# Second-MLP weights converted during the first MLP and kept in DRAM, and products chained in one PSUM bank

## The chip, the cores and the metric

The kernel runs on one core of a Trainium2 chip. TensorE (PE) multiplies into PSUM; ScalarE (ACT), VectorE (DVE) and GpSimd (POOL) work on tiles in SBUF, the first two also on PSUM; SyncE (SP) issues nearly all DMAs. The engines run side by side, each through its own instructions in a fixed order, and wait for one another by semaphores. The metric is the time of one execution in microseconds on the device; the median of several runs is compared.

## What is computed

Sliding-window attention (4 x 8 heads, 576 positions, window 128) gives 2304 tokens of 512 features. They pass two MLPs of 512 to 2048 to 512, one with an ELU and one with a leaky ReLU between its products:

```python
def _moe_ref(x, w_in, w_out):
    h = x @ w_in
    g = np.where(h > 0.0, h, 1.0 * (np.exp(np.minimum(h, 0.0)) - 1.0))
    return (g @ w_out).astype(np.float32)

def _moe2_ref(x, w_in, w_out):
    h = x @ w_in
    g = np.maximum(0.01 * h, h)
    return (g @ w_out).astype(np.float32)
```

The weights arrive as 64-bit words of two 32-bit halves, and the kernel turns them into fp32.

## The kernel before

**Number format.** Each fp32 operand is split into a high part, which PE's fp32r format holds, and a low rest: ACT copies (the high part), DVE subtracts (the rest). A product is three matmuls, high x high, high x low, low x high (`split_mm`, L256).

**Order.** Work is written down in program order and a scheduler at build time lays out every engine's queue: an instruction may move ahead of earlier ones if its operands and a free buffer allow. Instructions in `keep_in_program_order` stay behind all that was written before them on their engine. All matmuls are pinned so, and on ACT the copies of the transposed scores (`copies`, L438) and the two passes `w_a1` and `w_a2` (together `w_first`, L210) that begin the conversion of a weight tile. The queues of SP, DVE and POOL are in order too once they are laid out.

**MLP1.** It runs over five token blocks J of 512, 256, 512, 512 and 512 tokens. A block has 16 steps c, one for each 128 hidden features: `mlp1_h` (12 matmuls, then exp on ACT, two operations on DVE, a cast to the high part `gh` on ACT, the rest `gl` on DVE), and `mlp1_y` of two steps earlier (12 matmuls). In blocks 0 to 3 the attention of later tokens goes in between, in rounds: blocks 1 to 3 have 8 rounds each, at the start of the even steps. A round (L648 and below) is, on PE, `transposes` of two sets of scores (into the PSUM banks of the tags s1 and h, copied out by ACT), `values` of the round before, and `score_mm` of the next round (into s0 and s1). Blocks 0 to 2 end at about 152, 223 and 335 us, block 3 at 445, block 4 at 526. The weights of MLP1 are converted in block 0 (`w_tick`), which calls for no conversion in the step right ahead of a round.

**MLP2.** Both of its products are done by a scheme of seven products of half-size blocks instead of eight (after Strassen), over three groups of 768 tokens. First come 24 units u, 8 for each group (`unit_a`, `unit_b`, `unit_c`): 7 products of 6 matmuls with 384 columns each, accumulated in three banks, x (products 1, 2), y (6, 7, 4) and z (5, 3), with sums s1, a, b taken out by ACT and DVE; the results go through the leaky ReLU to DRAM (`g2T`). Then `second(n)` runs over 28 steps of 12 matmuls for each group (`SEQ`), its operands prepared four steps ahead by `prepare` (splits on ACT and DVE, differences of activations).

**Weights of MLP2 in the kernel before.** A pair of tiles (`pair_load`, 1 MB) is loaded, converted (`w_first`, a shift and an addition on DVE) and combined. The eight input pairs are converted in block 4 of MLP1, with four sums each on POOL; they stay in SBUF and are split as the units need them (`split_w`). The eight output pairs are converted during the last nine units, their sums are made on POOL (`sums`), and `prepare` splits them in the first group of `second`; one sum goes through DRAM (`s4T`) for want of room.

Of the kernel before, what the change touches and what calls it, by code (L numbers as in the profile page):

```python
# [98 lines left out]
def attention_elu_leaky_kernel(  # L99
# [150 lines left out]
    def weights(layer, c, io):  # L250
        while (layer, c) not in W:
            w_tick(NC * layer)
        w = W[layer, c]
        return w[:, io, 0], w[:, io, 1]

# [391 lines left out]

    for J in range(len(BLK1) - 1):  # L648
# [3 lines left out]
        for c in range(NC):  # L652
# [19 lines left out]
            pend.append((J, [c], g))  # L672
    values_to(NS - 1)
# [5 lines left out]
    S, H1, H2, OP, Xr, F, SUM = {}, {}, {}, {}, {}, {}, {}  # L679
    F_ORDER = [(j, 2 * h + q) for h in range(2) for j in range(2) for q in range(2)]  # L680
    s4T = dram.tile([P, NP2, 2 * P], F32, name="s4T")

    def pair_load(kind, i, home, tag):

        raw = home.tile([P, 2, DM, 2], I32, tag=tag, name="wraw")
        if kind == "in":
            src = w_in2[2 * i:2 * i + 2]
        else:
            j, q = F_ORDER[i]
            src = w_out2[j, 2 * q:2 * q + 2]  # L690
        src = src.bitcast(I32).rearrange("c p (n w) -> p c n w", w=2)
        for c in range(2):
            nc.sync.dma_start(out=raw[:, c], in_=src[:, c])
        raws[kind, i] = raw

    def pair_convert(kind, i):

        k = kind, i
        w_ts(k)
        raw, f = raws.pop(k), mids.pop(k)  # L700
        if kind == "in":
            s = wp.tile([P, 8, 2 * P], F32, tag=f"w{i}", name="s")
            to = s[:, 3:7].rearrange("p i n -> p (i n)").rearrange("p (c n) -> p c n", c=2)
        else:
            j, q = F_ORDER[i]
            h = q // 2
            if q % 2 == 0:
                F[j, h] = wp.tile([P, 4, DM], F32, tag=f"w{2 * h + j}", name="f")
            to = F[j, h][:, q % 2 * 2:q % 2 * 2 + 2]
        dve.tensor_tensor(to.bitcast(I32), f, raw[:, :, :, 0], op=ALU.add)  # L710
        if kind == "in":
            for o, x, y, op in ((0, 5, 6, ALU.add), (1, 0, 3, ALU.subtract), (2, 3, 5, ALU.subtract), (7, 4, 1, ALU.subtract)):
                pool.tensor_tensor(s[:, o], s[:, x], s[:, y], op=op)
            S[k] = s

    def block(i, j, q):

        return F[j, q // 2][:, q % 2 * 2:q % 2 * 2 + 2, i * 2 * P:(i + 1) * 2 * P]

    def sums(n, h):  # L720

        if n not in SUM:
            SUM[n] = wp.tile([P, NP2, 2 * P], F32, tag=f"w{3 + n}", name=f"s{n}")
        for q in (2 * h, 2 * h + 1):
            o = {m: x[:, 2 * q:2 * q + 2] for m, x in SUM.items()}
            x, y, op = {1: lambda: (block(1, 0, q), block(1, 1, q), ALU.add), 2: lambda: (o[1], block(0, 0, q), ALU.subtract),
                        3: lambda: (block(0, 0, q), block(1, 0, q), ALU.subtract),
                        4: lambda: (block(0, 1, q), o[2], ALU.subtract)}[n]()
            pool.tensor_tensor(o[n], x, y, op=op)

    def in_load(p):
        pair_load("in", p, *((wrawp, "wraw") if p % 2 else (l2, "xr")))

    def out_load(k):
        if k < NP2:
            pair_load("out", k, *((wp, "w15") if k % 2 else (wrawp, "wraw")))
# [87 lines left out]
    def unit_a(u):  # L824
        x, y, z = (psp.tile([P, HALF], F32, tag=tg[u % 2], name=nm)
                   for tg, nm in ((("s0", "s1"), "px"), (("h", "c"), "py"), (("y0", "y1"), "pz")))
        product(1, u, x, True)
        s1 = small(glp, "gh", "s1")
        nc.scalar.copy(s1, x)
        product(6, u, y, True)  # L830
        a = small(glp, "gl", "a")
        nc.vector.tensor_tensor(a, y, s1, op=ALU.add)
        product(5, u, z, True)
        ps2[u] = x, y, z, s1, a

    def unit_b(u):
        x, y, z, s1, a = ps2[u]
        product(2, u, x, False)
        c11 = small(glp, "gh", "c11")
        g2_out(u, 0, 0, c11, x)  # L840
        product(7, u, y, False)
        b = small(glp, "gl", "b")
        nc.vector.tensor_tensor(b, y, s1, op=ALU.add)  # L843
        c22 = small(egp, "eg", "c22")
        nc.vector.tensor_tensor(c22, z, b, op=ALU.add)  # L845
        g2_out(u, 1, 1, c22, c22)

    def unit_c(u):
        x, y, z, s1, a = ps2.pop(u)
        product(4, u, y, False)  # L850
        c21 = small(egp, "eg", "c21")
        nc.vector.tensor_tensor(c21, y, s1, op=ALU.add)  # L852
        g2_out(u, 1, 0, c21, c21)
        product(3, u, z, False)
        c12 = small(egp, "eg", "c12")
        nc.vector.tensor_tensor(c12, z, a, op=ALU.add)
        g2_out(u, 0, 1, c12, c12)
# [10 lines left out]
    def raw_load(g, role, q, cell):  # L868
# [5 lines left out]
    W_HOME = {1: ("w8", "w9"), 5: ("w12", "w13"), 6: ("w10", "w11"), 2: ("w0", "w2"), 7: ("w4", "w5"), 4: ("w7", "w6"),  # L874
              3: ("w1", "w3")}
    S4 = {}

    def weight(m, q):
        if m in (1, 2, 4):
            return block(int(m == 4), int(m > 1), q)  # L880
        if m == 3:
            return S4.pop(q)
        return SUM[{5: 1, 6: 2, 7: 3}[m]][:, 2 * q:2 * q + 2]

    def prepare(n):
# [5 lines left out]
        if g == 0:  # L891
            i = {(4, 2): 0, (4, 3): 1, (3, 0): 2, (3, 1): 3}.get((m, q))
            if i is not None:
                S4[i] = egp.tile([P, 2, 2 * P], F32, tag="eg", name="s4")
                nc.sync.dma_start(out=S4[i], in_=s4T[:, 2 * i:2 * i + 2])
            if q == 0:
                A2[m] = [wp.tile([P, NP2, 2 * P], F32R, tag=tg, name="a2") for tg in W_HOME[m]]
            split2(*(x[:, 2 * q:2 * q + 2] for x in A2[m]), weight(m, q))
        cell = {r: RAW4[g, r][q] for r in ("b11", "b12", "b21", "b22") if len(RAW4.get((g, r), ())) > q}
        hi, lo = CELLS[n % len(CELLS)]  # L900
# [18 lines left out]
    def second(n):  # L919
# [4 lines left out]
        chain = {1: "x", 2: "x", 6: "y", 7: "y", 4: "y", 5: "z", 3: "z"}[m]  # L924
        for p in range(2):
            if m in (1, 6, 5) and q == 0:
                tag = {"x": ("y2", "y3"), "y": ("h", "c"), "z": ("s0", "s1")}[chain][p]
                PS2[chain, p] = psp.tile([P, HALF], F32, tag=tag, name="p" + chain)
# [9 lines left out]
    def out_store(g, p, i, k, tile_):  # L938
        r, t0 = (2 * p + i) * P, g * GRP + k * HALF
        nc.sync.dma_start(out=out[r:r + P, t0:t0 + HALF], in_=tile_)  # L940

    def evacuate(g, m, p):
        x, y, z = (PS2.get((c, p)) for c in "xyz")
        if m == 1:
            OUT2["s", p] = small(glp, "gh", "s1")
            nc.scalar.copy(OUT2["s", p], x)
# [27 lines left out]
    for c in range(NC):  # L974
# [11 lines left out]
        if c == 9:  # L986
            x2_load(0)
# [139 lines left out]
```

## Time and profile before

| | us |
|---|---|
| median of 3 runs | 908.93 (907.86 to 910.12) |
| the profiled execution | 912.43 |
| its span in the trace | 910.7 |
| PE busy | 880.4 (97%) |
| DVE, ACT, POOL busy | 638.0, 487.0, 200.3 |

A busy PE is not PE at its peak, since matmuls are pipelined: its pace is read from the time that many matmuls took. What an engine's busy share means is read stage by stage, since the stages have different limits.

### The profile page before, as it was taken

How to read it: one execution, taken by the hardware profiler on the slowest of the kernel's cores; microseconds unless marked ns; L12 is line 12 of the kernel's file. 1: busy time of each engine (PE TensorE's matmuls, PEld its weight loads, DVE VectorE, ACT ScalarE, POOL GpSimd, SP SyncE). 2: the span in 40 equal slices, each digit the busy share in tenths (PEclk: the TensorE clock that was granted, in tenths of full speed). 3: DMA queues.
4: the chain of work that ended last, by engine and by line, in shares of the span. 5: the costliest groups of instructions: out<-in, count | busy, mean ns of one | idle time of the engine just before them, and what ended most of it. 6: DMA issues, size and time to landing. Idle time of an engine off the chain costs nothing. (4 is left out here: it accounts for less than half of the span.)

```text
span 910.7 us, 14397 instructions
## 1 busy us (share of the span) xinstructions
PE 880.4 (97%) x5077; PEld 772.1 (85%) x5077; DVE 638.0 (70%) x1296; ACT 487.0 (53%) x1049; POOL 200.3 (22%) x341
## 2 busy tenths in 40 slices
PE   8999999999999999999999999999988779999998
PEld 5578878998877878788888899999988769899998
DVE  6799865556454454443489667896889999785954
ACT  7888854444343443333366446766788543444442
POOL 5802223322232211221064000000016780000000
PEclk9999999999999999999999999999999899999999
DMA  9941323212110120100355043433688707527101
GB/s 333 340 160 62 116 88 98 65 53 78 40 47 24 44 90 24 47 10 1 102 197 187 1 168 123 164 122 108 222 274 249 237 0 214 179 75 223 50 1 70
DMA packets 65768, 106.72 MB, mean 117 GB/s; under 512 B 5920, under 2 KB 52256, under 8 KB 65568
## 3 DMA queue, kind: packets, MB, share of 16 engines
q1 hardware_dynamic: 65120, 104.75, 34.9%
q10 hardware_dynamic: 576, 1.05, 0.3%
q8 instruction: 40, 0.66, 0.3%
q14 instruction: 32, 0.26, 0.1%
HBM read 76.41 MB, written 29.36 MB: 116 GB/s over the span
## 5 line engine op out<-in xcount | busy, mean ns | idle before, releaser
L136 PE MATMUL h_ps<-x,w 128*128 128x512 f32 (+1 forms) x960 | 214.9, 372 | 0.9 <-ACT x L127 0.5
L136 PEld LDWEIGHTS h_ps<-x,w 128*128 128x128 f32 x960 | 166.0, 188 | 38.8 <-ACT x L127 4.0
L136 PE MATMUL y<-gh,w 128*128 128x512 f32 (+1 forms) x640 | 157.2, 368 | 0.0
L136 PEld LDWEIGHTS y<-gh,w 128*128 128x128 f32 x640 | 113.8, 189 | 20.0
L127 POOL TENSOR_SCALAR_AFFINE_SELECT pt<-pt 128x256 f32<-128x256 f32 (+1 forms) x112 | 45.2, 412 | 213.7 <-ACT pt L441 210.1
L127 POOL TENSOR_SCALAR t<-t,stat 128x128 f32<-128x128 f32 (+3 forms) x160 | 71.7, 461 | 90.5 <-DVE stat L127 86.3
L538 ACT ACTIVATE eg<-h_ps 128x512 f32<-128x512 f32 (+1 forms) x80 | 44.0, 550 | 82.5 <-PE h_ps L136 80.2
L860 ACT CAST cells<-raw 128x768 fp32r<-128x768 f32 x60 | 50.1, 837 | 66.9 <-PE py L136 28.9
L541 ACT CAST gh<-eg 128x512 fp32r<-128x512 f32 (+1 forms) x80 | 46.2, 578 | 73.7 <-DVE eg L540 73.2
L127 ACT ACTIVATE t<-t,stat 128x128 f32<-128x128 f32 (+2 forms) x160 | 62.6, 394 | 42.1 <-DVE t L127 29.6
L136 PE MATMUL py<-x,h 128*128 128x384 f32 x336 | 78.7, 338 | 5.1 <-DVE b L843 5.0
L136 PE MATMUL py<-cells,a 128*128 128x384 f32 x432 | 78.0, 336 | 3.3 <-DVE cells L861 3.2
L542 DVE TENSOR_TENSOR gl<-eg,gh 128x512 fp32r<-128x512 f32 (+1 forms) x80 | 54.3, 679 | 36.6 <-ACT gh L541 36.6
L136 PEld LDWEIGHTS py<-cells,a 128*128 128x128 f32 x432 | 74.9, 188 | 5.2 <-DVE cells L861 5.1
L136 PE MATMUL y<-gl,w 128*128 128x512 f32 (+1 forms) x320 | 78.7, 368 | 0.0
L539 DVE TENSOR_SCALAR eg<-eg 128x512 f32<-128x512 f32 (+1 forms) x80 | 32.9, 412 | 64.1 <-ACT eg L538 62.0
L861 DVE TENSOR_TENSOR cells<-raw,cells 128x768 fp32r<-128x768 f32 x60 | 56.6, 956 | 22.9 <-ACT cells L860 22.4
L136 PEld LDWEIGHTS py<-x,h 128*128 128x128 f32 x336 | 60.6, 190 | 5.8 <-DVE b L843 5.4
L136 PEld LDWEIGHTS y<-gl,w 128*128 128x128 f32 x320 | 56.9, 189 | 10.0
L136 PE MATMUL pz<-cells,a 128*128 128x384 f32 x288 | 55.5, 349 | 7.4 <-DVE cells L861 5.2
L136 PEld LDWEIGHTS pz<-cells,a 128*128 128x128 f32 x288 | 52.4, 197 | 9.4 <-DVE cells L861 6.5
L136 PE MATMUL pz<-x,h 128*128 128x384 f32 x240 | 54.6, 341 | 2.7 <-DVE c L845 1.8
(91 smaller groups left out, 1540.4 us busy)
## 6 DMA issues: line engine op xcount, KB each, us to landing
g2T<-c SPq DMA_DIRECT2D x96, 192.0 KB, 2.0
wraw<-in_w_in SPq DMA_DIRECT2D x32, 512.0 KB, 4.7
wraw<-in_w_out SPq DMA_DIRECT2D x32, 512.0 KB, 6.1
raw<-g2T SPq DMA_DIRECT2D x36, 384.0 KB, 3.9
qkr<-in_kT SPq DMA_DIRECT2D x28, 192.0 KB, 2.7
xr<-x2T SPq DMA_DIRECT2D x3, 1536.0 KB, 7.3
b<-g2T SPq DMA_DIRECT2D x12, 384.0 KB, 5.8
out<-c SPq DMA_DIRECT2D x24, 192.0 KB, 2.3
```

The costliest lines, as they stand in the source:

```text
L127: ins = f(*args, **kw)
L136: tc.keep_in_program_order(nc.tensor.matmul(*args, **kw))
L538: nc.scalar.activation(g[:, :m], ps, AF.Exp)
L539: nc.vector.tensor_scalar(g[:, :m], g[:, :m], 1.0, -1.0, op0=ALU.min, op1=ALU.add)
L541: nc.scalar.copy(hi[:, :m], g[:, :m])
L542: nc.vector.tensor_tensor(lo[:, :m], g[:, :m], hi[:, :m].bitcast(F32), op=ALU.subtract)
L860: nc.scalar.copy(hi, src)
L861: nc.vector.tensor_tensor(lo, src, hi.bitcast(F32), op=ALU.subtract)
```

## The change

- A generator `pair_jobs` converts the eight input and then the eight output pairs during blocks 1 to 3 of MLP1, one piece at the end of each step (`next(jobs)`). It makes the four sums on DVE. An input pair takes two pieces: its sums and its words go to DRAM as fp32 (`sT`). An output pair takes four: its eight blocks are also split there, four at a time, and go to DRAM as high and low parts (`hlT`, in runs of 256 values). The raw words of a pair and the two split tiles share the tag `wraw`, of which there is one buffer.
- Block 4 only loads the finished input weights (`s_load`), and the operands of the first units are made a little earlier.
- The units and `second` accumulate in other banks: x takes products 1, 6, 7 and 4, each time after the running sum was copied out; z takes 5 and 3, and w takes 2 alone. s1, b and c21 are plain copies on ACT, a is a plain copy on DVE.
- `second` loads its weights ready split (`hl_load`, 2 MB for each of seven products); `prepare` no longer splits weights, and the differences of the first group move from POOL to DVE. The loads are spread over the last units.

```diff
+    def pair_jobs():
+        pair_load(PAIRS[0])
+        for n, k in enumerate(PAIRS):
+            kind, i = k
+            following = PAIRS[n + 1] if n + 1 < len(PAIRS) else None
+            yield
+            w_first(k)
+            yield
+            w_ts(k)
+            raw, mid = raws.pop(k), mids.pop(k)
+            dve.tensor_tensor(mid, mid, raw[:, :, :, 0], op=ALU.add)
+            a = mid.bitcast(F32).rearrange("p c (i n) -> p (c i) n", i=2)
+            x12, x21 = (1, 2) if kind == "in" else (2, 1)
+            s = wfp.tile([P, 4, 2 * P], F32, tag="wf", name="sums")
+            dve.tensor_tensor(s[:, 0], a[:, x21], a[:, 3], op=ALU.add)
+            dve.tensor_tensor(s[:, 1], s[:, 0], a[:, 0], op=ALU.subtract)
+            dve.tensor_tensor(s[:, 2], a[:, 0], a[:, x21], op=ALU.subtract)
+            dve.tensor_tensor(s[:, 3], a[:, x12], s[:, 1], op=ALU.subtract)
+            if kind == "in":
+                nc.sync.dma_start(out=sT[:, i, 4:], in_=s)
+                nc.sync.dma_start(out=sT[:, i, :4], in_=a)
+                pair_load(following)
+                continue
+            for o, four in ((0, s), (4, a)):
+                yield
+                t = wrawp.tile([P, 2, 4, 2 * P], F32R, tag="wraw", name="hl")
+                nc.scalar.copy(t[:, 0], four)
+                nc.vector.tensor_tensor(t[:, 1], four, t[:, 0].bitcast(F32), op=ALU.subtract)
+                nc.sync.dma_start(out=hlT[:, :, o:o + 4, i], in_=t.bitcast(F32))
+            pair_load(following)
...
+    jobs = pair_jobs()
     for J in range(len(BLK1) - 1):
...
             pend.append((J, [c], g))
+            if J:
+                next(jobs, None)
...
+    def s_load(p):
+        t = wp.tile([P, 8, 2 * P], F32, tag=f"w{p}", name="s")
+        for o, i, n in ((0, 4, 3), (3, 0, 4), (7, 7, 1)):
+            nc.sync.dma_start(out=t[:, o:o + n], in_=sT[:, p, i:i + n])
+        S["in", p] = t
...
+    def unit(u):
+        if u < NU:
...
+            product(1, u, x, True)
+            s1 = small(glp, "gh", "s1")
+            nc.scalar.copy(s1, x)
+            product(5, u, z, True)
+        if u:
+            x_, z_, a_ = ps2.pop(u - 1)
+            product(4, u - 1, x_, False)
+            c21 = small(glp, "gl", "c21")
+            g2_out(u - 1, 1, 0, c21, x_)
+        if u < NU:
+            product(6, u, x, False)
+            a = small(glp, "gl", "a")
+            nc.vector.tensor_copy(a, x)
+        if u:
+            product(3, u - 1, z_, False)
+            c12 = small(egp, "eg", "c12")
+            nc.vector.tensor_tensor(c12, z_, a_, op=ALU.add)
+            g2_out(u - 1, 0, 1, c12, c12)
+        if u < NU:
+            product(2, u, w, True)
+            c11 = small(egp, "eg", "c11")
+            nc.vector.tensor_tensor(c11, w, s1, op=ALU.add)
+            g2_out(u, 0, 0, c11, c11)
+            product(7, u, x, False)
+            b = small(glp, "gh", "b")
+            nc.scalar.copy(b, x)
+            c22 = small(egp, "eg", "c22")
+            nc.vector.tensor_tensor(c22, z, b, op=ALU.add)
+            g2_out(u, 1, 1, c22, c22)
+            ps2[u] = x, z, a
...
+    def hl_load(m):
+        A2[m] = [wp.tile([P, NP2, 2 * P], F32R, tag=tg, name="a2") for tg in W_HOME[m]]
+        for i in (0, 1):
+            nc.sync.dma_start(out=A2[m][i].bitcast(F32), in_=hlT[:, i, IN_HL[m]])
...
-            split2(*(x[:, 2 * q:2 * q + 2] for x in A2[m]), weight(m, q))
...
-            eng = pool if g == 0 and m != 1 else dve
-            eng.tensor_tensor(cell[o], cell[x], cell[y], op=ALU.subtract)
+            dve.tensor_tensor(cell[o], cell[x], cell[y], op=ALU.subtract)
...
-        chain = {1: "x", 2: "x", 6: "y", 7: "y", 4: "y", 5: "z", 3: "z"}[m]
+        chain = {1: "x", 6: "x", 7: "x", 4: "x", 5: "z", 3: "z", 2: "w"}[m]
```

## Rows read from the trace of the kernel before

**Rows 1.** Stretches by stage: us, busy us (instructions) per engine, clock, DMA.

```profile
151.70:223.30 71.60, 71.60 (x596) 65.10 (x594) 42.44 (x166) 33.51 (x121) 21.24 (x56) 1.00 0.25 75
223.30:335.40 112.10, 112.04 (x651) 89.82 (x651) 55.39 (x186) 45.01 (x144) 26.65 (x70) 1.00 0.15 42
335.40:444.70 109.30, 109.30 (x594) 87.80 (x593) 49.47 (x141) 38.52 (x108) 19.03 (x46) 1.00 0.13 41
...
525.90:667.00 141.10, 140.44 (x810) 140.12 (x809) 111.19 (x176) 93.47 (x170) 0.00 (x0) 1.00 0.47 163
667.00:703.60 36.60, 33.78 (x189) 32.10 (x187) 34.86 (x48) 29.66 (x49) 16.62 (x10) 1.00 0.77 248
703.60:790.75 87.15, 70.13 (x349) 65.43 (x350) 80.17 (x78) 41.61 (x64) 38.48 (x19) 0.92 0.53 166
790.75:907.27 116.52, 116.49 (x673) 116.16 (x671) 84.35 (x103) 46.79 (x60) 0.00 (x0) 1.00 0.27 82
```

**Rows 2.** Timeline (start, duration, engine, line): PE's first product of MLP2.

```profile
525.87 0.51 PE L136 MATMUL px<-x,h 128*128 128x384 f32 x2
```

**Rows 3.** Timeline of PE: the longest wait, in brackets with its releaser.

```profile
708.59 2.29 PE L136 MATMUL py<-x,h 128*128 128x384 f32 x6 [5.04 <-DVE b L843]
```

**Rows 4.** Timeline of ACT, then PE, at a round in block 1.

```profile
177.49 0.41 ACT L541 CAST gh<-eg 128x256 fp32r<-128x256 f32 x1 [0.82 <-DVE eg L540]
178.78 0.81 ACT L441 COPY pt<-pt_ps 128x256 f32<-128x256 f32 x2 [0.88 <-PE av_ps L136]
...
179.02 1.10 PE L136 MATMUL s_ps<-qkr 64*128 64x256 f32 x8
```

**Rows 5.** Timeline of ACT, then PE, at a round in block 2.

```profile
249.84 0.62 ACT L541 CAST gh<-eg 128x512 fp32r<-128x512 f32 x1 [1.22 <-DVE eg L540]
251.79 0.81 ACT L441 COPY pt<-pt_ps 128x256 f32<-128x256 f32 x2 [1.34 <-PE av_ps L136]
...
252.04 1.46 PE L136 MATMUL s_ps<-qkr 64*128 64x256 f32 x12
```

**Rows 6.** Timeline: the second input pair, its load (SP) and conversion in block 4.

```profile
126.86 0.80 SPq L693 DMA_DIRECT2D wraw<-in_w_in  x2
...
454.53 0.63 ACT L541 CAST gh<-eg 128x512 fp32r<-128x512 f32 x1 [1.30 <-DVE eg L540]
455.06 1.14 ACT L182 ACTIVATE wf<-wraw 128x1024 f32<-128x1024 f32 x1
456.10 1.14 ACT L187 ACTIVATE wraw<-wraw 128x1024 int32<-128x1024 uint32 x1
457.64 1.23 DVE L127 CUSTOM_DVE_ANT_0 s<-wraw,wf 128x2048 uint16<-128x2048 uint16 x1 [0.17 <-DVE wf L127]
```

**Rows 7.** Timeline of ACT at a round in block 0.

```profile
92.77 1.10 ACT L441 COPY pt<-pt_ps 128x256 f32<-128x256 f32 x4 [1.75 <-PE av_ps L136]
94.03 1.14 ACT L182 ACTIVATE wf<-wraw 128x1024 f32<-128x1024 f32 x1
```

**Rows 8.** Groups by line: count | busy us, mean ns of one | idle before.

```profile
L861 DVE TENSOR_TENSOR cells<-raw,cells 128x768 fp32r<-128x768 f32 x60 | 56.6, 956 | 22.9 <-ACT cells L860 22.4
L127 DVE TENSOR_SCALAR wf<-wf 128x1024 int32<-128x1024 int32 x32 | 29.1, 910 | 1.1 <-ACT wf L182 1.1
L127 DVE TENSOR_TENSOR t<-t 128x256 f32<-128x256 f32 x48 | 19.4, 425 | 0.6
L829 ACT COPY s<-px 128x384 f32<-128x384 f32 x24 | 11.4, 474 | 4.8 <-DMA g2T<-c 2.4 <-DMA x2T<-ys 1.7 <-PE px L136 0.6
```

**Rows 9.** Landing of a pair's loads; ys, 1 KB runs; `s4T` store; a wait at 657-672.

```profile
DMA to landing us min/median/max: 3.7/4.1/4.6
...
DMA to landing us min/median/max: 4.0/4.1/4.1
...
s4T<-s SPq DMA_DIRECT2D x1, 1024.0 KB, 3.9
...
DVE c L845 <- DMA g2T<-c: 2.8, 1, 2.8
```

More of the change, by code (lines that the diff above doesn't have):

```diff
@@ L254, in weights, with pair_load @@
         return w[:, io, 0], w[:, io, 1]
+    sT = dram.tile([P, NP2, 8, 2 * P], F32, name="sT")
+    hlT = dram.tile([P, 2, 8, NP2, 2 * P], F32, name="hlT")
+    def pair_load(k):
+        if k not in PAIRS:
+            return
+        kind, i = k
+        raw = wrawp.tile([P, 2, DM, 2], I32, tag="wraw", name="wraw")
+        src = w_in2[2 * i:2 * i + 2] if kind == "in" else w_out2[:, i]
+        src = src.bitcast(I32).rearrange("c p (n w) -> p c n w", w=2)
+        for c in range(2):
+            nc.sync.dma_start(out=raw[:, c], in_=src[:, c])
+        raws[k] = raw
+    PAIRS = [(kind, i) for kind in ("in", "out") for i in range(NP2)]
+    def pair_jobs():
+        pair_load(PAIRS[0])
+        for n, k in enumerate(PAIRS):
+            kind, i = k
+            following = PAIRS[n + 1] if n + 1 < len(PAIRS) else None
[24 more added lines that the diff above has]
+            pair_load(following)
     def split_mm(ps, whi, wlo, xhi, xlo, first, last, **kw):
@@ L678, in attention_elu_leaky_kernel @@
     g2T = dram.tile([P, NC, NT], F32, name="g2T")
[L679 to L736, printed above, removed]
+    S, H1, H2, OP, Xr = {}, {}, {}, {}, {}
+    def s_load(p):
[3 more added lines that the diff above has]
+        S["in", p] = t
@@ L1050, in attention_elu_leaky_kernel @@
-    prepare(0)
-    prepare(1)
-    sums(2, 1)
-    sums(3, 1)
-    for h in range(2):
-        sums(4, h)
-    nc.sync.dma_start(out=s4T, in_=SUM[4])
-    unit_c(NU - 1)
-    for q, cell in enumerate(raw_cells(wrawp, "wraw", 2) + raw_cells(l2, "at0", 2)):
-        raw_load(0, "b22", q, cell)
-    for q, cell in enumerate(raw_cells(l2, "at1", 2) + raw_cells(wfp, "wf", 1) + raw_cells(wfp, "wf", 1)):
-        raw_load(0, "b21", q, cell)
-    for n in range(2, AHEAD):
-        prepare(n)
+            continue
@@ new lines, in attention_elu_leaky_kernel @@
+        if p == 1:
+            raw_cells("b11", l2, "xr", 4)
+            xa = quarters(x1p.tile([P, 10, HALF], F32R, tag="x1", name="cells"), 5)
+            CELLS += [(xa[0], xa[1]), (xa[2], xa[3])]
+        elif p == 2:
+            hl_load(1)
+        elif p == 3:
+            raw_cells("b12", wp, "w15", 2)
+            raw_cells("b12", wrawp, "wraw", 2)
+        elif p == 4:
+            hl_load(5)
+        elif p == 5:
+            prepare(0)
+            hl_load(6)
+        elif p == 6:
+            prepare(1)
@@ L1064, in attention_elu_leaky_kernel @@
+    hl_load(2)
+    raw_cells("b22", wp, "w14", 2)
+    hl_load(7)
+    xb = quarters(x1p.tile([P, 10, HALF], F32R, tag="x1", name="cells"), 5)
+    CELLS += [(xb[0], xb[1]), (xb[2], xb[3]), (xa[4], xb[4])]
+    prepare(2)
+    unit(NU)
+    raw_cells("b22", l2, "at0", 2)
+    raw_cells("b21", l2, "at1", 2)
+    for _ in range(2):
+        raw_cells("b21", wfp, "wf", 1)
+    prepare(3)
+    hl_load(4)
+    hl_load(3)
     FROM = {"b11": ("b21", (13, 14, 15, 20)), "b12": ("b12", (16, 17, 18, 19)), "b22": ("b11", (21, 22, 23, 24)),
```

129 lines of the change are left out of this document (28 added, 101 removed).

## The prediction

> **What bounds the kernel now.** I read the time by stages first: TensorE (PE) is busy all of each MLP1 stretch from 151.7 to 444.7 us and all of the second and third token groups of the second MLP's last products (116.49 of 116.52 us), at full granted clock; the one stretch with real gaps is 703.6 to 790.75 us, where PE is busy 70.13 of 87.15 us at a granted clock of 0.92, and VectorE (DVE) 80.17 us [rows 1]. So the kernel is a PE stream with one hole. The size of the hole follows from the pace: the last two groups are 672 products of 384 columns in 116.5 us, 0.1734 each [rows 1]; the second MLP has 24 units of 42 such products and 3 groups of 336, 2016 in all, so 349.5 us. They start at 525.87 [rows 2] and would end at 875.4; they end at 907.27 [rows 1]. **Some 32 us** are lost, which is all that the second MLP can give back. About 3 us of it lie at 667 to 703.6 (PE busy 33.78 of 36.6) [rows 1]; the rest begins with PE waiting 5.04 us for DVE [rows 3] and goes on while ACT, DVE and GpSimd prepare the weights and operands of the first group at the same time.
>
> **The change part by part.**
>
> *The hole.* In the stretch 703.6 to 790.75 the 28 weight splits, the sums on GpSimd, and the last conversions go; 12 subtractions come back to DVE at 0.96 us each, less than the splits took. What is left per group is what the second and third groups do already, and those run without a gap [rows 1]. So the hole closes, except for what is late next: transfers. Seven pairs of prepared weights are 14.7 MB, against 8.4 MB of raw weights and 2 MB of sums before, beside the same 6.3 MB of activations. Before, the DMA engines were 0.77 busy at 667 to 703.6, and one activation store that was late held DVE up for 2.8 us [rows 1, 9]. I leave 8 us of the 32 (bounds 3, today's small stalls alone, and 16, half the hole): **24 us gained**.
>
> *The chain in one bank.* x takes products 1, 6, 7 and 4; between two of them lie two others, 12 x 0.1734 = 2.08 us, in which the copy (0.47 us on ACT, [rows 8]) has to be read out; before there were three or four. In 525.9 to 667 DVE is busy 111 and ACT 93 of 141 us and PE has no gap [rows 1]; the change shifts 0.5 us per unit from DVE to ACT. Cost: none if the reader is at most 1.4 us behind; 0 to 12 us otherwise (half a microsecond per unit). I count 2 of the 8 us above. A page speaks against this edit: the Trainium skill, "Perfetto Trace Analysis", Optimizing Tensor Performance, wants independent matmul groups to rotate through different PSUM banks so that evacuation overlaps the next group. Here two other banks stand between each reuse, so the rows give no cost; by the rule the reuse would be exposed, which is the last rival below.
>
> *The conversion moved into MLP1: where the forecast is decided.* From 444.7 to 525.9 it hid under PE; nothing is gained by taking it out there (PE has no gap to lose in that stretch). It goes to 48 steps from 151.7 to 444.7, where every second step, the even ones, opens with a round of attention. The generator gives an input pair two steps and an output pair four, and with the first load on step 0 the two ACT passes of w_first (pinned in program order) fall on odd steps always: right behind the step's cast of g and right ahead of the next round's copies of the transposed scores, which are pinned behind them. Today these copies come straight after the cast, and PE starts the next scores into the same bank at once: cast 177.49, copies 178.78, scores 179.02 in block 1 [rows 4]; 249.84, 251.79 and 252.04 in block 2 [rows 5]. In block 0, where weights are prepared between rounds, the passes come after the copies (copies 92.77, pass 94.03) [rows 7]. How pinned and unpinned work differ is seen in block 4: the second input pair is loaded at 126.86, some 300 us before block 4, as soon as its buffer is free, but its passes wait for their place, right behind a step's cast: cast 454.53, passes 455.06 and 456.10 (to 457.24) [rows 6].
>
>  So from the start of the cast to the end of the second pass are 2.7 us with 512 columns and, by the shorter cast (0.41 for 0.63), 2.5 with 256; the next may start 0.1 before that end, as the second pass does before the first's. Copies that began 1.29 us after the cast's start (178.78 - 177.49) can now begin at 2.4, those at 1.95 (251.79 - 249.84) at 2.6: PE waits **1.1 us per pair in block 1, 0.65 in blocks 2 and 3**, even when everything has arrived: 8 x 1.1 + 8 x 0.65 = 14 us. Nothing behind it hides this, since PE has no other gap.
>
>  Then the one buffer: raw words of a pair, and the two halves of the split output weights, share the single slot of the pool wraw. An input pair closes a loop: passes 2.2, addition 1.3 with its start [rows 6], SyncE's issues with a 0.5 MB store and the attention loads ahead 1.5, two loads of 0.5 MB that land 4.6 us after the second issue 5.0 [rows 9], 1.0 of queueing in the DMA rings: 11.0 us (bounds 8.7 without any wait, 13 with DVE busy). DVE has 42.4 of 71.6 us in block 1, and seven pairs of 0.91 + 1.23 + 4 x 0.43 [rows 6, 8] bring it to 69, so some waits there are likely. PE's time for the same two steps is 71.6 / 8 = 8.95. The longer of the two sets the pace: 7 x (11.0 - 8.95) + 1.1 = **15.5 us** (9 to 29).
>
>  An output pair: passes 2.2, addition 1.3, four sums 1.7 [rows 6, 8], then twice copy 1.14 (the 1024 columns of a pass, [rows 6]), subtraction 1.3 (0.96 x 1024/768, [rows 8]) and a store of 1 MB, then the load 5.1. The trace has no such store: a 1 MB one with long runs landed in 3.9 us, and two of 256 KB with 1 KB runs, the run length here, in 4.0 to 4.1 [rows 9]. Between 3.9 and twice 4.1 I take 6.0, nearer to the short runs. Sum 27.2, and 3 for six hand-overs between queues that hold attention work (0 to 6): 30.2 us, bounds 23 and 35. PE's four steps are (112.1 + 109.3) / 8 = 27.7 us. 7 x (30.2 - 27.7) + 0.65 = **18 us** (5 to 52).
>
>  Nothing else there costs: POOL loses its sums, stores and loads add some 42 MB over 293 us to 40 to 75 GB/s [rows 1], DVE stays under its limit in blocks 2 and 3 (55 + 4 pairs of 6.4 of 112 us).
>
>  Sum: +15.5 + 18 - 24 = +9.5 us, 922 against the profiled execution's 912.43 (span 910.7 and 1.7 around it). The three runs have their median 3.5 us lower, at 908.93; I carry the difference over: **918 us**.
>
> **Rivals.** *Faster:* the loops through the one buffer close within PE's steps (the transfers land as in the emptier stretches), so only the 14 us of queue order and 2 of small waits are paid, and 28 us are gained: 897. For it: unpinned work floats far ahead in before [rows 6]; against it: the sum of an output pair's own durations is 27 of 27.7 us. It decides at a store of about 5.5 us with 1 us of waits. *Slow buffer:* the output loop takes 35 us, because ACT and DVE stand in order behind a copy that waits for its store: 7 x 7.3 + 15.5 - 24 = +43, 952. It is the slower side of the same mechanism, decided by how stores of 1 KB runs land. *The hole stays:* the prepared weights or activations arrive late at the switch, 20 us stay lost: +21.5, 930. For it the 0.77 of the DMA engines; against it that unpinned loads float. *The bank:* each of the three reuses of x per unit costs 0.3 us, 24 x 3 x 0.3 = 21.6 more, 940; the copies' 0.47 us against 2.08 speaks against it. [...]
>
> **How the numbers follow.** Forecast as above 0.42 (own range 903 to 930), faster 0.28, slow buffer 0.17, hole stays 0.09, bank 0.04. About 0.3%, 2.7 us, is what can be told from no change. Under 906.2: 0.25 of the faster case and 0.04 of the forecast, 0.29; within: 0.03 and 0.09, 0.12; over: the rest, 0.59. The range leaves out a tenth on either side: 896 to 946.
>
> **What would show it.** Right: in the new trace each odd step from 151.7 on has the two passes ahead of the copies, PE's longest waits in that stretch are scores <- ACT copies, some 1 to 3 us, 16 times, the three blocks take some 30 us longer than 293, and from the start of the second MLP to the end it is about 357 us. Queue order alone is right if the waits are 1.1 and 0.65; the buffer if ACT's passes wait for the load of wraw. Wrong: the three blocks take 293 us or little more (the passes would then have to stand elsewhere in ACT's queue), or PE still waits for DVE at the switch.

## The result and the profile after

The changed kernel takes a median of **915.62 us** against 909.85 for the kernel before on the same chips: ratio **1.006, 95% interval 1.0041 to 1.0079**, 5.8 us longer. The forecast was 918 with a range of 896 to 946. One of its 16 executions took 4432 us, at a mean granted clock of 0.18; the ratio leaves it out, and without it the median is 915.09. The profiled execution took 917.84 us, with a span of 916.2.

By stages the profile after reads as follows (us of the stretch, then busy us and instructions of PE, PEld, DVE, ACT and POOL, the granted clock of PE, the DMA engines' share and GB/s). The stretches are blocks 1, 2, 3 and 4 of MLP1, the units (two lines), and the three groups of `second` (two lines):

```profile
151.70:240.00 88.30, 77.44 (x595) 67.45 (x594) 64.92 (x213) 49.77 (x137) 30.17 (x56) 0.96 0.74 251
240.00:356.30 116.30, 114.90 (x651) 90.73 (x650) 76.40 (x217) 60.01 (x160) 35.72 (x70) 1.00 0.47 149
356.30:473.40 117.10, 114.94 (x603) 91.33 (x602) 73.77 (x176) 56.41 (x127) 23.37 (x46) 0.97 0.43 141
473.40:554.30 80.90, 80.36 (x355) 66.20 (x354) 38.50 (x60) 25.94 (x42) 0.00 (x0) 1.00 0.36 117
554.30:700.00 145.70, 142.83 (x807) 142.16 (x806) 103.54 (x159) 98.22 (x189) 0.00 (x0) 0.98 0.51 172
700.00:737.85 37.85, 36.19 (x205) 35.23 (x204) 21.18 (x34) 21.16 (x42) 0.00 (x0) 1.00 0.82 264
737.85:796.09 58.24, 58.24 (x337) 58.24 (x337) 44.12 (x54) 25.71 (x34) 0.00 (x0) 1.00 0.85 288
796.09:912.60 116.51, 116.48 (x672) 116.16 (x671) 80.74 (x97) 48.91 (x64) 0.00 (x0) 1.00 0.27 82
```

Read against [rows 1]: the hole at the switch to `second` is gone (58.24 of 58.24 us busy in its first group), and the 5.04 us wait of [rows 3] with it. MLP2 now lasts 912.6 - 554.3 = 358.3 us where it lasted 381.4: 23.1 us gained. Blocks 1, 2 and 3 last 321.7 us where they lasted 293.0: 28.7 us lost, 16.7 of them in block 1. Block 4 did not get shorter without its conversions: 80.9 us, where the kernel before has

```profile
444.70:525.90 81.20, 81.20 (x360) 67.22 (x359) 62.81 (x79) 43.92 (x60) 27.06 (x32) 1.00 0.36 123
```

The waits that PE's rows show, and what ended them (us in total, times, longest; first over blocks 1 to 4, then over MLP2):

```profile
PE s_ps L136 <- ACT pt L489: 14.3, 13, 2.3
...
PE px L136 <- ACT b L854: 3.3, 3, 1.7
PE px L136 <- ACT s L831: 1.2, 1, 1.2
```

A round of block 1 shows the mechanism, on ACT and then PE (start, duration, engine, line; in brackets the idle time ahead and its releaser):

```profile
203.20 0.41 ACT L589 CAST gh<-eg 128x256 fp32r<-128x256 f32 x1 [0.86 <-DVE eg L588]
204.96 1.12 ACT L182 ACTIVATE wf<-wraw 128x1024 f32<-128x1024 f32 x1 [1.36 <-DMA wraw<-in_w_in]
205.97 1.13 ACT L187 ACTIVATE wraw<-wraw 128x1024 int32<-128x1024 uint32 x1
207.00 0.63 ACT L489 COPY pt<-pt_ps 128x256 f32<-128x256 f32 x2
...
207.41 0.92 PE L136 MATMUL s_ps<-qkr 64*128 64x256 f32 x6 [2.25 <-ACT pt L489]
```

Where [rows 4] have the cast and then the copies, the two passes now stand in between, and they have waited 1.36 us for their words before they began. The copies come 3.8 us after the cast's start, not 1.29, and PE loses 2.25 us. In block 2 (the rows that answer [rows 5]) it is the fp32r copy of the split that stands there in the steps without passes:

```profile
254.61 0.62 ACT L589 CAST gh<-eg 128x512 fp32r<-128x512 f32 x1 [1.22 <-DVE eg L588]
255.61 1.05 ACT L299 CAST hl<-wf 128x1024 fp32r<-128x1024 f32 x1 [0.38 <-DMA hlT<-hl]
256.61 0.81 ACT L489 COPY pt<-pt_ps 128x256 f32<-128x256 f32 x2
```

### The profile page after: what moved, and what is told of

Same layout as the page of the kernel before. It is cut to its first block, busy times and chain, and to the rows that moved or that the text cites. A ratio compares the mean times of both kernels' runs of the same rounds, so it can differ in the third digit from the quotient of the medians.

```text
span 916.2 us, 14526 instructions
## 1 busy us (share of the span) xinstructions
PE 887.4 (97%) x5077; PEld 776.3 (85%) x5077; DVE 620.4 (68%) x1330; ACT 500.5 (55%) x1067; POOL 140.5 (15%) x281
## 4 chain that ended last, share of the span: by engine, by line
PE 82%; DMA 4%; ACT 3%; DVE 2%; issue 2%; SPq 0%; ACTq 0%; DVEq 0%
PE px L136 21%; PE h_ps L136 19%; PE y L136 19%; PE pz L136 10%; PE pw L136 5%; PE s_ps L136 4%; PE av_ps L136 3%; DMA wraw<-in_w_in 1%; PE pt_ps L477 1%; DMA x2T<-ys 1%; DMA g2T<-c 1%; ACT wraw L187 1%; DMA xr<-x2T 1%; ACT pt L489 1%; ACT wf L182 0%
## 5 line engine op out<-in xcount | busy, mean ns | idle before, releaser
L136 PEld LDWEIGHTS y<-gh,w 128*128 128x128 f32 x640 | 113.7, 189 | 21.0 <-ACT ys L617 1.0
L861 ACT CAST cells<-raw 128x768 fp32r<-128x768 f32 x84 | 70.4, 840 | 84.5 <-PE px L136 49.9
L862 DVE TENSOR_TENSOR cells<-raw,cells 128x768 fp32r<-128x768 f32 x84 | 79.4, 956 | 38.2 <-ACT cells L861 37.7
L136 PE MATMUL px<-x,h 128*128 128x384 f32 x432 | 99.7, 337 | 4.5 <-ACT b L854 3.3
L136 PE MATMUL px<-cells,a 128*128 128x384 f32 x576 | 101.8, 334 | 0.0
L136 PEld LDWEIGHTS px<-cells,a 128*128 128x128 f32 x576 | 100.0, 188 | 0.0
L586 ACT ACTIVATE eg<-h_ps 128x512 f32<-128x512 f32 (+1 forms) x80 | 44.1, 551 | 101.0 <-PE h_ps L136 95.5
L127 POOL TENSOR_SCALAR_AFFINE_SELECT pt<-pt 128x256 f32<-128x256 f32 (+1 forms) x112 | 60.4, 557 | 226.1 <-ACT pt L489 224.2
L136 PEld LDWEIGHTS px<-x,h 128*128 128x128 f32 x432 | 77.3, 189 | 6.2 <-ACT b L854 4.3
L752 ACT CAST h<-s 128x512 fp32r<-128x512 f32 (+1 forms) x72 | 49.6, 693 | 26.9 <-PE pz L136 24.6
L136 PE MATMUL s_ps<-qkr 64*128 64x256 f32 (+4 forms) x256 | 45.8, 377 | 14.8 <-ACT pt L489 14.8
L127 DVE CUSTOM_DVE_ANT_0 t<-s_ps,bias 128x256 f32<-128x256 f32 (+4 forms) x160 | 52.2, 369 | 4.8 <-PE s_ps L136 4.2
```

The lines of the kernel that those rows point to most:

```text
L127: ins = f(*args, **kw)
L136: tc.keep_in_program_order(nc.tensor.matmul(*args, **kw))
L586: nc.scalar.activation(g[:, :m], ps, AF.Exp)
L752: nc.scalar.copy(hi[:, a:b], s[:, a + o:b + o])
L861: nc.scalar.copy(hi, src)
L862: nc.vector.tensor_tensor(lo, src, hi.bitcast(F32), op=ALU.subtract)
```

## The experiments

Below, a block's length is the time between VectorE's last copies of `ys` of it and of the block before, and "the units" are the time from the first product of MLP2 to the first product of `second`; at 1008 x 0.1734 us the units hold 174.8 us of products. All medians stand beside 909.6 to 910.3 us for the kernel before, run with them. The four columns on the right are from the one profiled execution of each kernel, which can lie some us off its median: most for e11 (4.7 us longer), e4 (4.4 shorter), e10 (3.5 longer) and e7 (3.2 longer).

| kernel | median us | block 1 | block 2 | block 3 | units |
|---|---|---|---|---|---|
| before | 909.85 | 71.4 | 112.7 | 109.3 | 187.0 |
| after | 915.62 | 88.3 | 116.9 | 116.6 | 183.4 |
| e1 passes in the other step | 917.36 | 89.9 | 121.5 | 110.9 | 184.3 |
| e2 no loads | 908.43 | 80.6 | 117.1 | 115.5 | 181.5 |
| e3 both | 909.94 | 91.0 | 115.7 | 111.2 | 182.1 |
| e8 both, no sums | 909.73 | 88.4 | 115.5 | 110.5 | 182.3 |
| e4 banks of before | 908.20 | 84.8 | 117.1 | 113.3 | 177.2 |
| e5 input pairs in block 4 | 897.33 | 71.4 | 117.0 | 114.7 | 181.0 |
| e6 and pieces in the round | 889.14 | 71.5 | 113.9 | 109.2 | 182.8 |
| e7 and banks of before | 886.25 | 71.5 | 113.8 | 109.3 | 181.8 |
| e9 e6, own tile for ys | 884.36 | 71.5 | 113.9 | 109.3 | 177.8 |
| e10 e7, own tile for ys | 885.74 | 71.5 | 113.9 | 109.3 | 181.1 |
| e11 load first | 919.36 | 95.5 | 116.9 | 115.3 | 182.9 |
| e12 e11, no stores | 909.05 | 83.6 | 116.9 | 113.7 | 184.3 |

(e8 is the time of one execution; the units of before contain its wait of [rows 3].) The four causes held against one another are: the place of the passes in ACT's queue, the loop through the landing buffer, DVE's load, and in MLP2 the chain in one bank.

**e2: the loop taken away.** After the first input pair nothing is loaded: the next pairs take the words that lie there.

```diff
         kind, i = k
+        if kind == "in" and i:
+            raws[k] = last["raw"]
+            return
```

> The raw words of the first input pair are kept and converted eight times, the other seven input pairs are not loaded: the input part of the second MLP's weights is wrong, all other work is the same. The passes stay ahead of the copies. If the buffer's loop (load behind addition) is what made block 1 longer, block 1 falls from 88.3 to 72 to 74 us and the time by 14 or more. If the place in the queue alone costs 1.1 us per pair, block 1 is 80 to 82 and the time falls by 6 to 8, to about 908. Blocks 2 and 3 stay at 232 to 235 by both.

Ratio 0.9985 (0.9973 to 0.9997); 7.2 us less than the changed kernel. The block's window, and PE's waits in it:

```profile
151.70:232.30 80.60, 74.36 (x595) 65.19 (x594) 64.73 (x213) 49.16 (x138) 30.06 (x56) 1.00 0.53 183
```

```profile
PE s_ps L136 <- ACT pt L493: 6.2, 8, 0.9
```

With the words always there, the passes alone still cost block 1 9.2 us, about 1.1 for each of 8 pairs, and no single wait is over 0.9 us. The rest of the 16.9, 7.7 us, goes with the loads; up to 3.5 of it is PE's granted clock, which is 1.00 here and 0.96 in block 1 of the changed kernel.

**e1 and e3: the passes one step later.** In block 1 the generator starts one step later, so that the passes fall into the step that has a round in it and not ahead of one; all later pieces move by a step with them. e3 does it without loads too.

```diff
-            if J:
+            if J > 1 or (J and c):
                 next(jobs, None)
```

> The generator starts one step later, so the two ACT passes of a pair fall on even steps: still behind the step's cast, but no longer right ahead of a round's copies. Block 1 of the changed kernel took 88.3 us against 71.6 before, blocks 2 and 3 233.4 against 221.4. If the place in ACT's queue is the cost, block 1 goes to 72 to 75 us, blocks 2 and 3 to 222 to 226, and the time falls by 20 us or more, to about 893. If the one buffer paces block 1 (10.6 us from pair to pair against 8.95 that PE needs), block 1 stays at 84 to 88 and only blocks 2 and 3 gain, about 7: 908. My theory holds both to be there: the buffer lags 1.65 us per pair, 11.5 over seven, of which one step without a round, about 4.5, can be absorbed: block 1 76 to 80, total about 897.

> Both edits at once: the passes on even steps, and the seven input pairs not loaded (that part of the weights is wrong). If these two causes are all that lengthened block 1, it is 72 to 74 us, and PE waits for no copies there. If it stays above 77, a third cause is at work (VectorE, which has some 65 of 72 us to do, or transfers that come late). The time is about 892 to 895 by the first.

Both ratios say no gain over the kernel before: 1.0099 (1.0065 to 1.0133) and 1.0005 (0.9995 to 1.0015). Block 1 did not shrink, in e3 not even without loads. My expectation of e1 was plainly wrong, and that of e3 too. Part of it is the clock: its mean over block 1 is 0.94 in e1 and 0.92 in e3, where e2 has 1.00, so some 5 and 7 us of these two blocks are a slower PE (estimates, as if PE were busy throughout). PE's waits on `s_ps` disappear and come back at another product, in e3 as

```profile
PE av_ps L136 <- DVE eg L592: 13.2, 7, 2.3
```

The timelines of ACT, DVE and PE at one round of e3 show how:

```profile
192.15 1.16 ACT L182 ACTIVATE wf<-wraw 128x1024 f32<-128x1024 f32 x1
193.21 1.15 ACT L187 ACTIVATE wraw<-wraw 128x1024 int32<-128x1024 uint32 x1
194.26 0.36 ACT L590 ACTIVATE eg<-h_ps 128x256 f32<-128x256 f32 x1
...
194.40 1.23 DVE L127 CUSTOM_DVE_ANT_0 wf<-wraw,wf 128x2048 uint16<-128x2048 uint16 x1 [0.36 <-ACT wraw L187]
195.54 0.29 DVE L591 TENSOR_SCALAR eg<-eg 128x256 f32<-128x256 f32 x1
...
196.08 0.42 DVE L592 TENSOR_TENSOR eg<-h_ps,eg 128x256 f32<-128x256 f32 x1
...
196.55 0.88 PE L136 MATMUL av_ps<-pt,vr 128*64 128x128 f32 x12 [1.20 <-DVE eg L592]
```

The next step's exponential stands behind the passes on ACT, the two DVE operations behind it (the second reads the same hidden sums) stand behind the weight addition, and `av_ps` of the round is released by the second. So in block 1 PE pays for the 2.3 us of passes, and the addition of 1.23 behind them, in either step; only which product pays changes. In blocks 2 and 3 the shift helped, 226.9 us in e3 for 232.6 in e2; why is not shown here.

**e8: DVE's sums.** Three of the four sums of each input pair are left out of e3; both its stores take the words instead.

> The run with shifted steps and without the input loads, and three of the four sums of each input pair left out (that part of the weights is wrong; the stores are as many). There block 1 was 91 us, with PE waiting 14.7 us for VectorE to have read the odd step's bank before the next round's values. If VectorE's queue is the cause, 1.3 us less per pair gives 80 to 84 us and waits of 5 to 9; if the two passes on ACT are (exp of the odd step stands behind them), block 1 stays at 88 to 91.

```profile
PE av_ps L136 <- DVE eg L597: 13.4, 7, 2.3
```

Block 1 is 88.4 where it was 91.0, and the waits are as before: DVE's sums are not what PE waits for.

**e5: the input pairs out of blocks 1 to 3.** They are converted in block 4 again, as in the kernel before, but with their sums on DVE; the generator handles only output pairs.

```diff
-    PAIRS = [(kind, i) for kind in ("in", "out") for i in range(NP2)]
+    PAIRS = [(kind, i) for kind in ("out",) for i in range(NP2)]
...
-            if J:
+            if J > 1:
```

> Undoes one part: the input pairs are converted in block 4 as in the kernel before (sums on VectorE, kept in SBUF), and the generator does the output pairs alone, from block 2 on. If it is the input pairs that lengthened block 1 (88.3 us against 71.6), block 1 is 71 to 73, blocks 2 and 3 stay at 230 to 234, block 4 stays at 80 to 82 with VectorE some 70 us busy, and the time falls by about 16, to 899. Against it: if preparation costs PE the same wherever it stands, block 4 grows by what block 1 gives back and the time stays at 912 to 916.

Ratio 0.9868 (0.9848 to 0.9889). Block 1 is back at 71.4 us, and block 4 stays at 81.0 us: the conversion had been free there. 18.3 us of the changed kernel's time is the input pairs' move; 16.9 of it is seen in block 1. e5 also makes the first units' operands as late as the kernel before does, and its units are 2.4 us shorter.

**e6: pieces behind the copies.** This is e5, and for the even steps the generator's piece is called inside the round, after the copies of the transposed scores. (The first load comes at the end of block 1.)

```diff
-            if J > 1:
+            if J > 1 and c % 2 or J == 1 and c == NC - 1:
                 next(jobs, None)
...
                     w_tick(NC)
+                if J > 1:
+                    next(jobs, None)
```

> As the run before, and the pieces of the even steps stand inside the round, behind the copies of the transposed scores, so the two ACT passes of an output pair come where ACT waits for the next scores (2.2 us in the trace of before). If the place of the passes is what lengthened blocks 2 and 3 by 12 us, they go from 233 to 221 to 225 and the time to about 889. If the one buffer's loop is it, they stay at 230 to 234 and the time at 899; if VectorE's added work is it (some 40 us per block), they stay above 228.

Ratio 0.9775 (0.9749 to 0.9801), another 8.2 us. In ACT's timeline the copies follow the cast again as in [rows 5], and the fp32r copy comes after them:

```profile
251.58 0.62 ACT L589 CAST gh<-eg 128x512 fp32r<-128x512 f32 x1 [1.35 <-DVE eg L588]
253.44 0.81 ACT L489 COPY pt<-pt_ps 128x256 f32<-128x256 f32 x2 [1.24 <-PE av_ps L136]
...
255.39 1.05 ACT L299 CAST hl<-wf 128x1024 fp32r<-128x1024 f32 x1 [0.87 <-DMA hlT<-hl]
```

The output pairs' work is the same, with the same loads, stores and single buffer, so neither the loop's length nor DVE's added work lengthened blocks 2 and 3 by itself. What the loop did there was to hold the fp32r copy longer in front of the transposed scores: in blocks 2 and 3 of the changed kernel ACT waits 4.6 us, in 7 such copies, for the store of the one before. e6 has such waits too (0.87 us above), but behind the copies. Where a wait hides in a record, the group's busy time shows it: the group of `s_ps` products in block 2 (count, busy us, mean ns, idle ahead), in the changed kernel and then in e6, is

```profile
L136 PE MATMUL s_ps<-qkr 64*128 64x256 f32 (+3 forms) x80 | 13.2, 357 | 1.3 <-ACT pt L489 1.3
```

```profile
L136 PE MATMUL s_ps<-qkr 64*128 64x256 f32 (+3 forms) x80 | 10.4, 354 | 0.0
```

2.8 us of busy time and 1.3 of idle make 4.1 of the 4.2 us by which block 2 had grown.

**e4, e7, e9, e10: the units.** In e4 the units' sums lie in the banks of the kernel before (its three functions `unit_a`, `unit_b`, `unit_c` instead of `unit`, so that the small tiles `gh`, `gl` and `eg` are dealt out as there too); e7 is e6 with the same. In e9 and e10, which are e6 and e7 otherwise, the last block's four `ys` tiles have a tile of their own:

```diff
+            own = wrawp.tile([P, NK, n], F32, tag="wraw", name="ysl") if J == len(BLK1) - 1 else None
             for i, y in enumerate(Y.pop(J)):
-                if i == 3:
+                if own is not None:
+                    ys = own[:, i:i + 1]
+                elif i == 3:
```

> The 24 units take their sums as in the kernel before (x for products 1 and 2, y for 6, 7 and 4, z for 5 and 3, three or four products between two uses of a bank instead of two); the rest is the changed kernel. The units took 183.6 us against 174.8 without a gap. If the short chain in one bank is what lost the 8.8 us, they take 175 to 177 and the time falls by 6 to 8, to about 908.5. If late transfers alone lost them (a store of the first MLP's result that took 9 us, weight loads beside stores), the units stay at 181 to 184 and the time within 2 us of the changed kernel's.

> As the run before, and the 24 units take their sums in the banks of the kernel before, with three or four products between two uses. With the units alone changed they fell from 183.6 to about 177 us; if that adds up with the rest, the time is about 883, below both kernels. If the units' gaps came from transfers that have moved by now, the time is that of the run before.

> The version with the input pairs in block 4 and the pieces inside the round took 889.1 us, and its units 182.8 us from the first unit to the first product of the cells, of which 174.8 are products. Here the last block's four ys tiles lie in a tile of their own, so that their stores, which land some 7 us behind the large activation load, no longer hold the buffers that the first unit's VectorE writes. If those stores hold up the units: units about 178 us, time about 885 us. If the chain of products in one bank alone makes the 8 us: units unchanged at 182 to 183 us, time 889 us.

> The version with the units' sums in the banks of the kernel before took 886.3 us, its units 181.8 us, and the last block's ys stores held the units' buffers there as well. With a tile of their own for ys: if the stores and the bank are two separate losses, units 176 to 178 us and time 882 to 884 us; if a later wait (the switch's subtraction behind an activation load) takes their place, units above 180 us and time 886 us.

e4: ratio 0.9992 (0.997 to 1.0015), units 6.2 us shorter. That looks like the price of the chain, and I took it for that until e9: with the chain kept and only the `ys` tiles moved, the units fall from 182.8 to 177.8 and the time to 884.36 (0.9709, 0.9694 to 0.9725). What the first unit ran into is in the changed kernel's rows, on DVE and then PE:

```profile
561.93 0.56 DVE L850 TENSOR_TENSOR c<-pw,s 128x384 f32<-128x384 f32 x1 [3.74 <-DMA x2T<-ys]
...
563.46 1.32 PE L136 MATMUL px<-x,h 128*128 128x384 f32 x6 [1.70 <-ACT b L854]
565.94 1.01 PE L136 MATMUL px<-x,h 128*128 128x384 f32 x2 [1.16 <-ACT s L831]
```

and in the landings (KB each, median us) of the last block's stores and of the load issued ahead of them:

```profile
xr<-x2T SPq DMA_DIRECT2D x2, 1536.0 KB, 8.0
x2T<-ys ACTq DMA_DIRECT2D x2, 256.0 KB, 8.3
x2T<-ys SPq DMA_DIRECT2D x2, 256.0 KB, 9.6
```

The stores hold the buffers that the first unit's sums want; DVE stands 3.74 us, ACT's copies come late, and PE, whose products keep their order, comes to the same bank again two products later. With the banks of before the stores landed as late (8.3 and 9.6 us in the kernel before, 8.3 and 9.5 in e4), and PE waited 1.4 us in all the units of e4, where the changed kernel has 4.5. In e9 they land no earlier either (8.5 and 9.9), but hold no buffer that a unit wants, and PE's waits in the units are

```profile
PE px L136 <- ACT b L872: 1.4, 2, 0.8
PE px L136 <- DVE a L859: 0.4, 1, 0.4
```

so the chain as such costs at most the 3.0 us by which 177.8 exceeds 174.8. The clock had a share here as well: its mean over the units is 0.98 in the changed kernel, 0.99 in e6 and 1.00 in e4 and e9, so that of the 5 to 6 us some 3 are waits and most of the rest is a slower PE. Together the two cures do not add up: e7, expected at 883, is not clear of e6, and e10 (0.9723, 0.9695 to 0.9752) is where e7 is (0.9746, 0.9714 to 0.9778). There another wait sets the units, DVE first and then PE:

```profile
703.07 0.96 DVE L127 TENSOR_TENSOR raw<-raw 128x768 f32<-128x768 f32 x1 [4.16 <-DMA raw<-g2T]
703.95 0.55 DVE L861 TENSOR_TENSOR b<-py,s 128x384 f32<-128x384 f32 x1
...
704.55 1.97 PE L136 MATMUL py<-x,h 128*128 128x384 f32 x5 [4.15 <-DVE b L861]
```

A difference for `second`, whose activations land late, stands in DVE's queue ahead of a sum that PE needs. It is the wait of [rows 3] with another cause.

**e11 and e12: what closes the loop in block 1.** In e11 the next input pair's load is issued behind the addition, ahead of the sums and the two stores; e12 also leaves out the stores of seven pairs.

```diff
             a = mid.bitcast(F32).rearrange("p c (i n) -> p (c i) n", i=2)
+            if kind == "in":
+                pair_load(following)
...
                 nc.sync.dma_start(out=sT[:, i, 4:], in_=s)
                 nc.sync.dma_start(out=sT[:, i, :4], in_=a)
-                pair_load(following)
```

> The changed kernel with one edit: the following input pair's load is issued right behind the addition of the two passes, ahead of the three sums and the two stores. Block 1 took 88.3 us there: some 9 us over the kernel before from the place of the passes in ScalarE's queue alone, and some 8 from the loop through the one landing buffer and the lower granted clock. If the loop sets these last microseconds, it gets some 1.5 us shorter for each pair: block 1 at 82 to 85 us, waits for the landed pair gone, time 911 to 913 us. If the loop does not set them, block 1 stays at 87 to 89 us and the time at 915 us.

> The version with the load ahead of the stores, and seven of the eight input pairs are not stored to DRAM (the first MLP2 product then uses the first pair for all, so the output is not the reference's). With the load first, block 1 took 96.1 us instead of 88.3, since ScalarE's pass waited 7.1 us for the store of the buffer wf, which landed in 7.0 us behind the loads instead of 3.3. If the loop of an input pair closes through two buffers, wraw (its load) and wf (its store), neither the order of load and store nor one of them alone can shorten it, and without the stores only the place of the passes is left: block 1 at 80 to 83 us, no wait of a pass for a store or a load, time 908 to 911 us. If the stores do not matter: block 1 at 88 to 96 us, time 915 to 919 us.

e11 did neither of what was expected: 1.009 (1.0053 to 1.0127), block 1 at 95.5 us (the 96.1 that e12's expectation names counts from a copy earlier). By the time alone it is not clear of the changed kernel, whose interval is 1.0041 to 1.0079, and its profiled execution is a long one, at a low clock in block 1:

```profile
152.03:248.10 96.07, 82.46 (x598) 71.94 (x596) 66.03 (x214) 50.57 (x139) 29.98 (x56) 0.91 0.70 230
```

At 0.91 for 0.96 the clock is some 5 of the 7.2 us by which the block grew. What is shown is that the new order brought no gain. A wait of ACT says why:

```profile
ACT wf L182 <- DMA sT<-wf: 7.1, 5, 2.6
```

and the landings (KB each, median us) go with it:

```profile
wraw<-in_w_in SPq DMA_DIRECT2D x14, 512.0 KB, 5.9
...
sT<-wf SPq DMA_DIRECT2D x8, 512.0 KB, 7.0
```

In the changed kernel the same two views have a wait for the load and a faster store:

```profile
ACT wf L182 <- DMA wraw<-in_w_in: 4.1, 5, 1.4
```

```profile
wraw<-in_w_in SPq DMA_DIRECT2D x14, 512.0 KB, 5.4
sT<-wf SPq DMA_DIRECT2D x8, 512.0 KB, 3.3
```

A pass needs two things: its words in `wraw`, and a free buffer of the tag `wf`, which the pair before holds until it is stored. The rows fit a loop that is closed by whichever of load and store is issued second. Without the stores, e12 is back at 909.05 us (0.9988, 0.9969 to 1.0007), 10.3 below e11 and 6.6 below the changed kernel, and PE waits 7.8 us in block 1, 1.6 at the longest. Its block 1, 83.6 us, is 0.6 above what was expected, and the time is as expected; passes still wait 1.4 us for a store or a load (three times). The reading through two buffers holds so far as it goes: taking away the loads (e2) or the stores (e12) shortens block 1, changing their order does not. How much of e12's gain is the buffer and how much the emptier DMA engines (0.54 busy, for 0.70 in e11 and 0.74 in the changed kernel) it does not tell apart.

## Why the prediction was right, and where not

- **The hole.** 24 us of 32 were to come back; 23.1 did. The 8 us that were to stay did (358.3 - 349.5 = 8.8), but not where I put them: the switch has no gap at all, at a DMA share of 0.82 to 0.85, and nearly all of the loss (183.4 - 174.8 = 8.6) lies in the units.
- **The chain in one bank.** 2 us (0 to 12) were counted. e9 bounds the chain itself at 3.0 us, so the term was about right; the other 5 or so come from a step that I did not make: whose buffers the units' sums take over. The late stores were in the kernel before as well, where PE waited 0.7 us in all for the copies of s1; the change exposed them. The rival that had each reuse exposed at 0.3 us (21.6 us) is refuted. The prediction also read too much into a rule: the Trainium skill, "Perfetto Trace Analysis", Optimizing Tensor Performance, asks that independent matmul groups rotate through different PSUM banks so that the readout of one overlaps the next group. That the reuse would be exposed was my own conclusion: two products in other banks stand between each reuse here, so the readout does overlap the next product. What the runs show is that little is lost while the readers are on time (3.0 us at most), and 6.2 us with the late stores (the changed kernel against e4).
- **The passes ahead of the copies.** 1.1 us a pair were counted in block 1, 8.8 in all, and 9.2 were measured (e2). The longest waits (up to 2.3 us), the releaser and the length of the three blocks (28.7 us more, "some 30" told) are as described; the rows show 13 such waits for the 16 told. In blocks 2 and 3 I counted 0.65 for each of 8 pairs, 5 us; e6 gives 8.2 in the time. What failed there is that I placed only the passes: the fp32r copies of the split stand ahead of the copies of other rounds in the same way.
- **The input pairs' loop.** +15.5 us were told for block 1 and 16.9 measured (13.4 in the profiled execution of e4, whose block 1 is the same code); 18.3 in the time (e5). The loop was put at 11.0 us a pair; block 1 took 88.3 / 8 = 11.0. The loads landed in 5.4 us for the 4.6 that the sum took. No row shows its 1.0 of queueing or its 1.5 of issues by themselves, and the clock's share stands in no term, so that the whole agrees to a tenth is in part luck. The buffer that I closed it through is only one of two (e11, e12).
- **The output pairs' loop** is the step that was wrong. I had 30.2 us for it, longer than PE's 27.7, and took +18 from that. e6 runs the same loop in (113.9 + 109.2) / 8 = 27.9 us, which is PE's pace to within 0.2, so it did not set the pace; the store, put at 6.0 us, landed in 5.3 (4.8 in e6). On this step the faster rival had it right. Blocks 2 and 3 became 11.5 us longer all the same, for the two reasons above and below. In the profile the parts are 16.9 + 11.5 - 23.1 = +5.3 us, where the sum had 15.5 + 18 - 24 = +9.5: a largest cost that was not there was in good part made up by what had been left out, and so far the nearness of 918 is luck.
- **Left out: the clock.** In block 3 PE's granted clock fell, to the lower of its two levels (1.2 and 2.4 GHz) for some us, where PE had just waited (stretches of 5 us):

```profile
355.00:360.00 5.00, 3.68 (x30) 2.59 (x28) 3.11 (x6) 3.82 (x6) 0.00 (x0) 1.00 0.66 249
360.00:365.00 5.00, 4.51 (x12) 3.28 (x13) 4.50 (x16) 2.76 (x12) 1.97 (x4) 0.52 0.42 118
365.00:370.00 5.00, 5.00 (x19) 4.05 (x18) 2.58 (x7) 2.33 (x5) 1.35 (x3) 0.80 0.00 0
```

  and PE's timeline there:

```profile
360.49 1.86 PE L136 MATMUL s_ps<-qkr 64*128 64x192 f32 x6 [1.82 <-ACT pt L489]
362.28 5.20 PE L136 MATMUL h_ps<-x,w 128*128 128x512 f32 x12
```

  Twelve products of 512 columns took 5.2 us; at the pace of [rows 1] they are 12 x 0.1734 x 512/384 = 2.8. If PE was busy all the while, the mean of 0.97 over 117.1 us cost block 3 some 3.5 us, 0.96 over 88.3 block 1 as much, and 0.98 over 183.4 the units about as much again (estimates). Not every wait brings it on: of six stretches of 13 to 15 us in block 1, with eight waits, two show 0.89 and four 1.00. It is not the same in every execution either: e4, whose MLP1 is that of the changed kernel, had block 1 at 84.8 us with a clock of 0.98. And it goes with the times: of the changed kernel's executions the two at a mean clock of 0.996 took 910.7 and 910.8 us, the three at 0.985 to 0.987 took 918.4 to 918.9. PE's gaps are therefore not the whole price of a wait.
- **"Nothing else there costs"** was not borne out for the transfers. Traffic in block 1 went from 75 to 251 GB/s, the DMA share from 0.25 to 0.74, and a pair's loads landed in 5.4 us for 4.1 [rows 9]. What that cost by itself no run tells.

By medians the steps from e6 to the changed kernel are these: e6, which has hardly anything left of the two losses in MLP1, stands 20.7 us under the kernel before; the input pairs in block 1 take 18.3; the place of the output pairs' pieces takes 8.2; together +5.8. (They must add up, being the steps of one chain of runs.) The change's idea was sound and its placing cost more than it gained: with the input pairs left where they were free, the pieces behind the copies, and a tile for the last stores, the kernel takes 884.36 us (e9), 25.9 less than the kernel before run with it (910.30).

What stays open is how block 1's 7.7 us beyond the place of the passes divide among the two buffers, the busier DMA engines and the clock.

## What to carry to other kernels

Before moving work under a stage that has PE full, look up in the trace which short operation on each in-order engine releases PE, and put the moved work behind it, never between it and its input; if every gap between such operations is shorter than the moved work, leave it where it is free. For each buffer that changes hands across the seam of two stages, name the DMA that frees it and what is queued ahead of that DMA. A loop through buffers is only as short as the last of all the buffers that its first step needs.

## What the runs showed of the hardware

- Stores of 256 KB that land in 2.8 us in block 1 of the kernel before took 8.3 to 9.6 us at the end of block 4, there as in the changed kernel, where a 1.5 MB load had been issued about 1 us ahead of them; from ACT's queue it was 8.3, from SP's 9.6. This agrees with the Trainium skill, "DMA: Bandwidth & Descriptors", Issuing engines are not separate DMA queues, by which transfers run on the same 16 DMA engines whoever issues them.
- Issuing a pair's load ahead of its stores (e11) moved the landing of the store of `wf` from 3.3 to 7.0 us and made the load no faster (5.4 and 5.9).
- After a stretch in which PE was busy 3.68 of 5 us, and a wait of 1.82, came some 6 us at a granted clock near half, the lower of its two levels (1.2 and 2.4 GHz). By the means of 0.52 and 0.80 over 5 us each that took away some 3.4 us of PE's work (an estimate), nearly twice the wait itself.
